# The order of the last sigmoids and of one block's final sums in a fused attention and gated feed-forward kernel

## The chip, the cores and the metric

The kernel runs on one core of one Trainium2 chip. The metric is the device time of one execution in microseconds (us); a lower figure is better. The core's engines work side by side: TensorE (PE) multiplies matrices, with its weight loads shown apart as PEld; VectorE (DVE), ScalarE (ACT) and GpSimd (POOL) do elementwise work; SyncE (SP) issues transfers, as the queues of ACT and POOL can too. Each engine takes its instructions in the order of the program and waits for the others through semaphores.

## The reference

The inputs q, k and v have the shape (8, 8, 576, 64): batch, head, token, head dimension. There are four weight matrices and one vector of gains.

```python
kv  = einsum('bhsd,bhse->bhde', k, v)          # per batch and head, 64 x 64
o   = einsum('bhsd,bhde->bhse', q, kv)
t   = o / sqrt(mean(o * o, -1) + 1e-6)         # per token and head
x   = (t * g_norm), heads side by side         # 4608 tokens x 512
g   = x @ w_gate                               # 512 x 1536
ffn = (gelu(g) * (x @ w_val)) @ w_out          # 1536 x 512
out = x + sigmoid(x @ w_res) * ffn             # float32
```

The result has 4608 rows of 512 numbers. For every one of them the sigmoid's gate multiplies the feed-forward output, and x is added.

## The kernel before, in words

**Blocks.** The tokens are worked on in nine blocks of 512: blocks 0 to 7 hold the first 512 tokens of each of the eight batches, and the last block, number 8, holds the remaining 64 tokens of each batch. A block has four groups of rows j = 0 to 3, each of 128 tokens (one a partition) by 512 columns. For each block there is a stage for gate and value (the hidden rows `hid`, in float16), a stage for the residual gate (`x @ w_res`, kept as a tanh in `th_all`), and the output stage. The attention of later batches is woven in between.

**Fewer products.** From block 1 on, the output stage forms the product with `w_out` in a scheme of seven products instead of eight: rows and columns are halved into quarters, and sums of hidden rows (`hid_s`) and of weights (`wo_ts`) are multiplied. Gate and value (function `gv_group`, from block 2 on in groups of four slices of 128 hidden columns) and, in the last blocks, the residual gate (`res_halves`) are formed in the same way. A product of this kind is written with `prod` or `product`, each into a PSUM bank; intermediate results (called A, D, E, F, c, d) are added by DVE and copied by ACT.

**The final sums.** `out_by_products` makes the output stage of blocks 1 to 7. `pf` (L636) multiplies the gate with the product into `res_all`; the profile calls this tile `osb`. `fin` (L640) adds x, which is in `t_t`, on POOL; `store` (L645) issues the transfer to the output on SP. A pair (jj, ch) names a quarter: jj = 0 is the rows j = 0 and 1, jj = 1 the rows j = 2 and 3; ch is the half of the columns. For block 1 alone (`later`) the sums aren't made at the end of the stage but are put into block 2's first group of gate and value products. They need x there, which at that moment is `t` without the gains: `a_x` (L355) multiplies one group of rows with the gains `g16` on DVE.

**How the work is placed.** The order is written out by hand: `gv_group` runs through a list of words, and `at_word(block, group, word, ...)` hangs further steps behind a word. For a group that is not the block's last one, the list is

```python
False: "1g 1v Eg 5g Ev 5v dg 6g dv 6v Fg 2g Fv 2v 7g g11 7v cg 3g cv 3v h11 g12 4g g21 h12 4v g22 h21 h22",
```

A word with a digit is a product (1 to 7, for gate or value); E and d are copies on ACT (L872, L876), F and c are sums on DVE (L883), g with two digits is a gelu on ACT (L893), h the hidden quarter on DVE, or on POOL for 22 (L899). The two sums `cg` and `cv` read the banks A of gate and value, which the products 4g and 4v write next. Each step is issued at its place to its own engine's queue, so an operation stands behind all that was issued to that engine before.

**The last block.** `out_last` makes the residual gate and the output of block 8. `res_halves` runs through the words `1 sE 5 sd 6 +F 2 tE 7 +c 3 tF 4 tc tA`: digits are products on PE, `sE` and `sd` copies on ACT, `+F` and `+c` sums on DVE, and `tE`, `tF`, `tc`, `tA` tanhs on ACT (L561). `tA` reads the last product in the bank that `wf` takes over. A sigmoid is half a tanh plus one half: `m_sigmoid(j)` (L429) makes it in place for one group of rows of all 512 columns. `half_d(0)` and `half_d(1)` are the two halves of product D; ACT copies D to `d` (L739). Then PE forms the products of A, E, F and A twice more; DVE adds `d` into `wf` (L463), and multiplies each product with its sigmoid (`gated`, L700); `plus` (L704) adds x, on POOL or DVE; `store` (L709) halves each transfer between the SP and the ACT queue. For the lower right quarter, rows j = 2 and 3 of the second half of the columns, POOL forms `u` = sigmoid * d + x ahead (L463, two instructions), and DVE adds it to the gated product (L463).

Of the kernel before, what the change touches and what calls it, by code (L numbers as in the profile page):

```python
# [8 lines left out]
FP32 = mybir.dt.float32  # L9
FP16 = mybir.dt.float16  # L10
I32 = mybir.dt.int32
AF = mybir.ActivationFunctionType
# [6 lines left out]
def kernel(  # L19
# [407 lines left out]
    def m_sigmoid(j):  # L427
        th = th_all[:, j, :]
        nc.scalar.activation(out=th, in_=th, func=AF.Copy, scale=0.5, bias=0.5)  # L429
# [154 lines left out]
    def out_by_products(blk, later, banks, amid):  # L584
        w = {}
        s_ = hid_sums

        def aside(ahead_of):
            for f in amid.get(ahead_of, ()):
                f()  # L590

        def res(jj):
            for j in (2 * jj, 2 * jj + 1):
                m_res(blk, j, banks[j])

        def tiles_of_w():
            for n in ("D", "E", "F", "A"):
                w[n] = pmoe.tile([P, 2, CH], FP32, name="w" + n, bank=banks[n])
            w["d"] = attnp.tile([P, 2, CH], FP32, tag="sq", bufs=3, name="wd")

        def half(n, e, a, b):
            prod(w[n][:, e : e + 1], a, b, e == 0, (e,))

        def half_d(e):
            half("D", e, s_[0], wo_t[:, 0])

        def with_res():
            res_halves(blk, dict(zip("AFE", (banks[j] for j in range(3)))), {
                "sd": [tiles_of_w, lambda: half("A", 0, a_of(blk, 1, 1), b_of(1, 1)), lambda: s_sum(blk, 0)],
                "+F": [lambda: half("A", 1, a_of(blk, 1, 1), b_of(1, 1)), lambda: s_sum(blk, 1),  # L610
                       lambda: nc.scalar.copy(out=w["E"], in_=w["A"])],
                "+c": [lambda: s_sum(blk, 2), lambda: s_sum(blk, 3)],
                "tF": [lambda: half_d(0)],
            })
            half_d(1)
            nc.scalar.copy(out=w["d"], in_=w["D"])
            for j in range(NJ):
                m_sigmoid(j)

        def first_two():  # L620
            tiles_of_w()
            s_last(blk)
            prod(w["A"], a_of(blk, 1, 1), b_of(1, 1), True)
            nc.scalar.copy(out=w["E"], in_=w["A"])
            aside("D")
            prod(w["D"], s_[0], wo_t[:, 0], True)
            nc.scalar.copy(out=w["d"], in_=w["D"])
            aside("gates")
            for j in range(NJ):
                m_sigmoid(j)  # L630

        def part(jj):
            return slice(None), slice(2 * jj[0], 2 * jj[0] + 2), slice(jj[1] * CH, (jj[1] + 1) * CH)

        def pf(jj, src, eng=nc.vector):
            eng.tensor_tensor(out=res_all[part(jj)], in0=th_all[part(jj)], in1=src, op=ALU.mult)  # L636

        def fin(jj):
            of = part(jj)
            nc.gpsimd.tensor_tensor(out=res_all[of], in0=res_all[of], in1=t_t[blk][of], op=ALU.add)  # L640

        def store(jj):
            dst = out[blk * S : blk * S + M0, :].rearrange("(p j) c -> p j c", j=NJ)
            js = slice(2 * jj, 2 * jj + 2)
            nc.sync.dma_start(out=dst[:, js, :], in_=res_all[:, js, :])  # L645

        def others():


            prod(w["A"], s_[1], wo_t[:, 1], False)  # L650
            aside("F")
            sub(nc.vector, w["F"], w["A"], w["d"], ALU.add)
            aside("00")
            prod(w["E"], a_of(blk, 1, 2), b_of(2, 1), False)
            pf((0, 0), w["E"])
            aside("22")
            prod(w["A"], s_[2], wo_t[:, 2], False)
            c22 = res_all[part((1, 1))]
            sub(nc.vector, c22, w["A"], w["d"], ALU.add)
            aside("01")  # L660
            prod(w["F"], s_[3], b_of(2, 2), False)
            pf((0, 1), w["F"])
            aside("11")
            prod(w["A"], a_of(blk, 2, 2), wo_t[:, 3], False)
            if whole(blk + 1):
                pf((1, 1), c22, nc.gpsimd)
                pf((1, 0), w["A"])
            else:
                pf((1, 1), c22)
                pf((1, 0), w["A"])  # L670
            if later:
                return
            for i in (1, 0):
                fin((i, i))
                fin((i, 1 - i))
                store(i)

        if later:
            x = [lambda j=j: a_x(blk, j) for j in range(NJ)]
            at_word(blk + 1, 0, "1v", *x[0:2])  # L680
            at_word(blk + 1, 0, "Fv", x[2])
            at_word(blk + 1, 0, "cv", x[3], lambda: fin((0, 0)), lambda: fin((0, 1)), lambda: store(0))
            at_word(blk + 1, 0, "h22", lambda: fin((1, 0)), lambda: fin((1, 1)), lambda: store(1))
        if res_in_halves(blk):
            return [with_res, lambda: None, lambda: None, others]
        return [lambda: res(0), lambda: res(1), first_two, others]

    def out_last(blk, banks):
# [3 lines left out]
        def bank(n, i):  # L692
            return pmoe.tile([P, n, CH], FP32, name="w", bank=i)

        def part(j, n, ch):
            return slice(None), slice(j, j + n), slice(ch * CH, (ch + 1) * CH)
# [9 lines left out]
        def store(j, n, c0, c1):  # L706
            for e, queue in enumerate((nc.sync, nc.scalar)):
                dst = out.rearrange("(j e s) c -> e s j c", e=2, s=S)[e, M0:S, j : j + n, c0:c1]
                queue.dma_start(out=dst, in_=res_all[e * R : (e + 1) * R, j : j + n, c0:c1])  # L709

        def run():
            wa, w = [], []
            one = (slice(0, 1), slice(1, 2))

            def ahead(e):
                if e == 0:
                    wa.extend(bank(1, banks["A"][e]) for e in range(2))
                    w.extend(bank(2, banks[n]) for n in "DE")
                prod(wa[e], a_of(blk, 1, 1), b_of(1, 1), True, (e,))

            def seed():
                for e in range(2):
                    nc.scalar.copy(out=w[1][:, one[e], :], in_=wa[e])

            def half_d(e):
                prod(w[0][:, one[e], :], s_[0], wo_t[:, 0], e == 0, (e,))

            res_halves(blk, dict(zip("AFE", (banks[j] for j in range(3)))), {
                "sd": [lambda: ahead(0), lambda: s_sum(blk, 0)],
                "+F": [lambda: ahead(1), lambda: s_sum(blk, 1), seed],  # L730
                "+c": [lambda: s_sum(blk, 2), lambda: s_sum(blk, 3)],
                "tF": [lambda: half_d(0)],
            })
            wd, we = w
            wf = bank(2, banks["F"])
            d = attnp.tile([P, 2, CH], FP32, tag="sq", bufs=3, name="wd")
            u = attnp.tile([P, 2, CH], FP32, tag="sq", bufs=3, name="u")
            half_d(1)
            nc.scalar.copy(out=d, in_=wd)  # L739
            for j in (2, 3, 0, 1):  # L740
                m_sigmoid(j)
            for e in range(2):
                prod(wa[e], s_[1], wo_t[:, 1], False, (e,))
                sub(nc.vector, wf[:, one[e], :], wa[e], d[:, one[e], :], ALU.add)
            sub(nc.gpsimd, u, th_all[part(2, 2, 1)], d, ALU.mult)
            sub(nc.gpsimd, u, u, t_t[blk][part(2, 2, 1)], ALU.add)
            prod(we, a_of(blk, 1, 2), b_of(2, 1), False)
            gated(0, 2, 0, we)
            plus(0, 2, 0, nc.gpsimd)
            store(0, 2, 0, CH)  # L750
            prod(wf, s_[3], b_of(2, 2), False)
            gated(0, 2, 1, wf)
            plus(0, 2, 1, nc.gpsimd)
            store(0, 2, CH, C)
            for e in range(2):
                prod(wa[e], s_[2], wo_t[:, 2], False, (e,))
                gated(2 + e, 1, 1, wa[e])
            of = part(2, 2, 1)
            sub(nc.vector, res_all[of], res_all[of], u, ALU.add)
            store(2, 2, CH, C)  # L760
            for e in range(2):
                prod(wa[e], a_of(blk, 2, 2), wo_t[:, 3], False, (e,))
                gated(2 + e, 1, 0, wa[e])
                plus(2 + e, 1, 0, nc.vector)
            store(2, 2, 0, CH)
# [531 lines left out]
    def at_word(blk, i, word, *fs):  # L1297
        amid_gv.setdefault((blk, i), {}).setdefault(word, []).extend(fs)
# [252 lines left out]
```

## Time and profile before

| what | value |
|---|---|
| median of 9 runs | 323.91 us (323.62 to 324.31) |
| the profiled execution's own time | 323.91 us |
| its span, first to last instruction | 322.1 us |
| mean granted clock of TensorE | 0.997 |
| instructions | 7558 |
| last product of PE ends | 315.9 us |
| last DVE operation ends | 318.0 us |

Times of single instructions count from the start of the span. The page of a profile gives the busy time of each engine, a chain of waits followed back from the last instruction, and groups of instructions by line, operation and tile. A group's entry shows the number of instructions, the mean length of one and what ended the idle time before it; the timeline shows them one after the other. An operation's tiles are named by the program: `osb<-osb,t` writes `osb` and reads `osb` and `t`. Some operations go through a helper and bear its line: sums through `sub` are on L463.

### The profile page before, as it was taken

What the parts mean: (1) busy time and instruction counts of PE and PEld (TensorE: products, weight loads), DVE (VectorE), ACT (ScalarE), POOL (GpSimd) and SP (SyncE); (2) the same over time, 40 slices, a digit from 0 to 9 for tenths busy, and PEclk for the clock granted to TensorE, in tenths of its full rate; (3) what the DMA queues carried; (4) which work ended last, traced back from release to release, by engine and by line L of the source; (5) the groups of instructions that cost most, each with busy time, mean ns of one, the idle gap of its engine ahead of it and who ended that gap; (6) DMA issues with size and microseconds to landing.
All of it is one profiled execution on the core that took longest, in us unless ns stands there. A gap on an engine that the chain in (4) does not pass through costs nothing.

```text
span 322.1 us, 7558 instructions
## 1 busy us (share of the span) xinstructions
PE 313.5 (97%) x2972; PEld 240.2 (75%) x2972; DVE 271.5 (84%) x492; ACT 203.7 (63%) x373; POOL 144.9 (45%) x212
## 2 busy tenths in 40 slices
PE   8999999999999999999999999999999999999992
PEld 3545755444857878887888688868888888888881
DVE  5788879799799888998899889999998777877774
ACT  3773685365727784878487848684767467737760
POOL 2792341573712779337843784117511332051232
PEclk9999999999999999999999999999999999999998
DMA  7999999798995599399938893810321030012004
GB/s 254 326 204 204 194 205 182 167 189 124 158 136 102 177 134 96 133 164 120 111 132 160 109 127 131 137 32 2 130 47 36 2 130 4 2 52 80 0 2 130
DMA packets 76693, 38.89 MB, mean 121 GB/s; under 512 B 42098, under 2 KB 74354, under 8 KB 76658
## 3 DMA queue, kind: packets, MB, share of 16 engines
q0 software_dynamic: 38752, 17.17, 42.6%
q1 hardware_dynamic: 37328, 20.71, 24.7%
q8 instruction: 23, 0.38, 0.5%
q10 hardware_dynamic: 578, 0.52, 0.5%
q14 instruction: 12, 0.10, 0.1%
HBM read 38.80 MB, written 9.44 MB: 150 GB/s over the span
## 4 chain that ended last, share of the span: by engine, by line
PE 95%; DVE 3%; issue 0%; ACT 0%; DVEq 0%; ACTq 0%
PE Ag L862 11%; PE Av L862 11%; PE wA L500 11%; PE rps L415 7%; PE gps L395 6%; PE vps L395 6%; PE Fv L862 6%; PE Fg L862 6%; PE fps L432 3%; PE Eg L862 3%; PE wF L500 3%; PE Ev L862 3%; PE wE L500 3%; PE wD L500 3%; PE w L500 2%; PE idle L1027 2%
## 5 line engine op out<-in xcount | busy, mean ns | idle before, releaser
L899 POOL TENSOR_TENSOR hid<-ge,c 128x512 f16<-128x512 f16 x21 | 24.5, 1165 | 68.7 <-ACT ge L893 48.7
L640 POOL TENSOR_TENSOR osb<-osb,t 128x512 f32<-128x512 f32 x28 | 31.5, 1157 | 35.2 <-DVE osb L636 24.3
L500 PEld LDWEIGHTS <-hid_s 128*128 128x128 f16 x384 | 37.6, 98 | 4.3
L862 PEld LDWEIGHTS <-wsv 128*128 128x128 f16 x336 | 32.8, 98 | 4.0
L862 PEld LDWEIGHTS <-wsg 128*128 128x128 f16 x336 | 32.8, 98 | 3.8
L500 PEld LDWEIGHTS <-hid 128*128 128x128 f16 x288 | 28.2, 98 | 4.3
L872 ACT COPY Eg<-Ag 128x512 f32<-128x512 f32 x21 | 12.2, 582 | 25.9 <-PE Ag L862 25.9
L383 ACT ACTIVATE ge<-gps 128x512 f16<-128x512 f32 x24 | 14.1, 597 | 21.3 <-PE gps L395 21.2
L862 PEld LDWEIGHTS <-wg 128*128 128x128 f16 x252 | 24.4, 98 | 3.7 <-issue 0.4
L862 PEld LDWEIGHTS <-wv 128*128 128x128 f16 x252 | 24.6, 98 | 3.3 <-issue 0.2
L883 DVE TENSOR_TENSOR Fg<-Ag,d 128x512 f32<-128x512 f32 x21 | 14.6, 697 | 13.3 <-ACT d L876 7.8
L862 PE MATMUL Ag<-ts,wsg 128*128 128x256 f16 x168 | 25.2, 273 | 0.0
L862 PE MATMUL Av<-ts,wsv 128*128 128x256 f16 x168 | 25.2, 272 | 0.0
L254 DVE TENSOR_REDUCE ss<-sq 128x8 f32<-128x512 f32 x32 | 20.1, 678 | 5.4 <-ACT sq L249 5.4
L395 PE MATMUL gps<-xT,wg 128*128 128x512 f16 x88 | 22.6, 379 | 0.0
L415 PE MATMUL rps<-wr,xT 128*128 128x512 f16 x96 | 22.6, 380 | 0.0
L395 PE MATMUL vps<-xT,wv 128*128 128x512 f16 x88 | 22.6, 379 | 0.0
L500 PE MATMUL wA<-wo_ts,hid_s 128*128 128x256 f16 x168 | 20.6, 273 | 0.0
L384 DVE TENSOR_TENSOR hid<-ge,vps 128x512 f16<-128x512 f16 x24 | 16.2, 683 | 4.8 <-PE vps L395 4.0
L429 ACT ACTIVATE th<-th 128x512 f32<-128x512 f32 x36 | 20.0, 641 | 0.0
L355 DVE TENSOR_TENSOR t<-t,g 128x512 f16<-128x512 f16 x36 | 19.7, 575 | 0.0
L893 ACT ACTIVATE ge<-Eg 128x512 f16<-128x512 f32 x21 | 12.5, 597 | 10.5 <-PE Eg L862 10.5
(209 smaller groups left out, 797.1 us busy)
## 6 DMA issues: line engine op xcount, KB each, us to landing
out_dram<-osb SPq DMA_DIRECT2D x14, 512.0 KB, 2.6
qraw<-in_q_dram POOLq DMA_DIRECT2D x7, 512.0 KB, 7.1
k<-in_k_dram POOLq DMA_DIRECT2D x7, 512.0 KB, 8.6
v<-in_v_dram POOLq DMA_DIRECT2D x7, 512.0 KB, 10.9
wg<-in_moe_w_gate_dram POOLq DMA_DIRECT2D x2, 512.0 KB, 8.2
wv<-in_moe_w_val_dram POOLq DMA_DIRECT2D x2, 512.0 KB, 8.7
wo<-in_moe_w_out_dram POOLq DMA_DIRECT2D x2, 512.0 KB, 13.7
out_dram<-osb SPq DMA_DIRECT2D x4, 256.0 KB, 4.5
```

Source lines behind the costliest of these rows:

```text
L254: nc.vector.tensor_reduce(out=out_, in_=sqs.pop((b, i)), op=ALU.add, axis=mybir.AxisListType.X)
L355: eng.tensor_tensor(out=t_t[blk][:, jj, :], in0=t_t[blk][:, jj, :], in1=g16, op=ALU.mult)
L383: nc.scalar.activation(out=ge, in_=gps, func=AF.Gelu)
L384: nc.vector.tensor_tensor(out=hids[blk][:, f, :], in0=ge, in1=vps, op=ALU.mult)
L395: nc.tensor.matmul(ps[:, j0 * P : j1 * P], lhsT=w[:, cc, :], rhs=xT_t[blk][:, j0:j1, cc, :], start=(cc == 0 and j0 == 0), stop=(cc == NP - ...
L415: nc.tensor.matmul(rps, lhsT=xT_t[blk][:, j, cc, :], rhs=wr16[:, cc, :], start=(cc == 0), stop=(cc == NP - 1),)
L429: nc.scalar.activation(out=th, in_=th, func=AF.Copy, scale=0.5, bias=0.5)
L500: nc.tensor.matmul(ps[:, e - es[0], :], lhsT=a[:, f, e * P : (e + 1) * P], rhs=b[:, f, :], start=(start and e == es[0] and f == 0), stop=( ...
L640: nc.gpsimd.tensor_tensor(out=res_all[of], in0=res_all[of], in1=t_t[blk][of], op=ALU.add)
L862: nc.tensor.matmul(out_[:, r, :], lhsT=lhsT, rhs=rhs, start=(first and r == 0 and c == 0), stop=(c == 1), skip_group_check=True,)
L883: nc.vector.tensor_tensor(out=dst, in0=ps["A", u], in1=sb["d", u], op=ALU.add)
L899: eng.tensor_tensor(out=dst, in0=ge[q], in1=source(q, "v"), op=ALU.mult)
```

## The change

There are two parts.

In the first, the sums of block 1 that stand in block 2's first group are exchanged. Behind the word `cv`, after the fourth multiplication with the gains, there are now the two sums and the store of the rows jj = 1; behind `h22` those of the rows jj = 0.

In the second, the last block's sigmoids are made by quarter (two groups of rows, half of the columns) instead of by group of rows, and in another order. The lower right quarter comes directly behind its tanh `tc`, then the second half of product D and the copy of it to `d`, and only then the tanh `tA`; the other three quarters follow. PE's products keep their order.

```diff
-            at_word(blk + 1, 0, "cv", x[3], lambda: fin((0, 0)), lambda: fin((0, 1)), lambda: store(0))
-            at_word(blk + 1, 0, "h22", lambda: fin((1, 0)), lambda: fin((1, 1)), lambda: store(1))
+            at_word(blk + 1, 0, "cv", x[3], lambda: fin((1, 0)), lambda: fin((1, 1)), lambda: store(1))
+            at_word(blk + 1, 0, "h22", lambda: fin((0, 0)), lambda: fin((0, 1)), lambda: store(0))
...
+            kept = []
+
+            def keep_d():
+                kept.append(attnp.tile([P, 2, CH], FP32, tag="sq", bufs=3, name="wd"))
+                nc.scalar.copy(out=kept[0], in_=w[0])
+
+            def sigmoid(j, ch):
+                th = th_all[part(j, 2, ch)]
+                nc.scalar.activation(out=th, in_=th, func=AF.Copy, scale=0.5, bias=0.5)
+
...
                 "tF": [lambda: half_d(0)],
+                "tc": [lambda: sigmoid(2, 1), lambda: half_d(1), keep_d],
             })
             wd, we = w
+            (d,) = kept
             wf = bank(2, banks["F"])
-            d = attnp.tile([P, 2, CH], FP32, tag="sq", bufs=3, name="wd")
             u = attnp.tile([P, 2, CH], FP32, tag="sq", bufs=3, name="u")
-            half_d(1)
-            nc.scalar.copy(out=d, in_=wd)
-            for j in (2, 3, 0, 1):
-                m_sigmoid(j)
+            for j, ch in ((0, 0), (0, 1), (2, 0)):
+                sigmoid(j, ch)
```

## The prediction

> **What bounds the kernel now.** I read the page first: TensorE (PE) works through nearly the whole span, and of the chain that ended last 95% is PE and 3% VectorE (DVE).
>
> ```profile
> PE 313.5 (97%) x2972; PEld 240.2 (75%) x2972; DVE 271.5 (84%) x492; ACT 203.7 (63%) x373; POOL 144.9 (45%) x212
> PE 95%; DVE 3%; issue 0%; ACT 0%; DVEq 0%; ACTq 0%
> ```
>
> So a change gains only where PE stands still, or behind PE's last product. I asked who waited for whom on PE from 97 us to the end. One line came back:
>
> ```profile
> PE Ag L862 <- DVE c L883: 0.2, 1, 0.2
> ```
>
> The timeline of that place, in block 2's first group of gate and value products (columns: start, length, engine, line, operation; an x2 is two instructions merged), explains it:
>
> ```profile
> 100.26 2.27 POOL L640 TENSOR_TENSOR osb<-osb,t 128x512 f32<-128x512 f32 x2 [10.61 <-DVE t L355]
> 101.54 1.27 DVE L355 TENSOR_TENSOR t<-t,g 128x512 f16<-128x512 f16 x1
> 102.74 0.68 DVE L883 TENSOR_TENSOR c<-Ag,d 128x512 f32<-128x512 f32 x1
> 103.34 0.67 DVE L883 TENSOR_TENSOR c<-Av,d 128x512 f32<-128x512 f32 x1
> 102.69 0.60 PE L862 MATMUL Fv<-xT,wsv 128*128 128x256 f16 x4
> 103.47 0.60 PE L862 MATMUL Ag<-ts,wg 128*128 128x256 f16 x4 [0.18 <-DVE c L883]
> 104.06 0.60 PE L862 MATMUL Av<-ts,wv 128*128 128x256 f16 x4
> 104.50 0.60 PE L862 MATMUL Ag<-xT,wg 128*128 128x256 f16 x4
> ```
>
> PE starts a product of four matmuls every 0.44 us (104.06 to 104.50). From Fv to Ag it takes 0.78, from Ag to Av 0.59: 0.34 + 0.15 = 0.49 us lost. Ag and Av overwrite the banks that the two `c` sums read, and those sums stand behind a multiplication `t<-t,g` that took 1.27 us; the other seven of its kind nearby have a median of 0.416. It ended at 102.81, 0.28 after POOL's pair of adds (100.26 + 2.27 = 102.53).
>
> The second place is the end (timeline again):
>
> ```profile
> 309.41 0.59 ACT L739 COPY wd<-w 128x512 f32<-128x512 f32 x1
> 309.89 2.19 ACT L429 ACTIVATE th<-th 128x512 f32<-128x512 f32 x4
> 311.12 1.28 POOL L463 TENSOR_TENSOR u<-th,wd 128x512 f32<-128x512 f32 x1 [6.91 <-ACT th L429]
> 312.47 1.16 POOL L463 TENSOR_TENSOR u<-u,t 128x512 f32<-128x512 f32 x1
> 313.59 2.27 POOL L704 TENSOR_TENSOR osb<-osb,t 128x512 f32<-128x512 f32 x2
> 313.34 1.08 DVE L700 TENSOR_TENSOR osb<-th,w 128x512 f32<-128x512 f32 x2 [0.54 <-PE w L500]
> 315.17 1.24 DVE L463 TENSOR_TENSOR osb<-osb,u 128x512 f32<-128x512 f32 x1
> 316.33 0.41 DVE L700 TENSOR_TENSOR osb<-th,w 128x256 f32<-128x256 f32 x1
> ```
>
> The chain in order of time leaves PE at 314.62 and then runs on DVE alone to 317.98, before the last stores. Its longest link is the 1.24 us sum at 315.17. An add or multiply of that size with both inputs in SBUF takes 0.68 when POOL is idle:
>
> ```profile
> 90.47 0.68 DVE L636 TENSOR_TENSOR osb<-th,osb 128x512 f32<-128x512 f32 x1
> ```
>
> POOL's last add ran until 313.59 + 2.27 = 315.86; the DVE sum ended 0.55 later, at 316.41.
>
> **What the Trainium skill says.** "SBUF — State Buffer", section "Who interferes with whom": a DVE instruction with two SBUF inputs contends with a POOL instruction that reads SBUF, and the one that comes second blocks fully; with at most one SBUF input outside the two-port modes it does not. The trace agrees with both halves: both long DVE operations have two SBUF inputs and end a fraction after POOL's add, while Fg<-Ag,d (one input in PSUM) took 0.70 during POOL's adds at 100.34, as the sum rF<-rA,rd did at 305.77 with POOL idle. No other page carries a number that I need.
>
> **Part 1, the sums of block 1 in block 2.** Nothing is added or removed: still four POOL adds of 1.16 us and two stores, in the other order. The first pair, rows 1, now also needs the multiplications x[2] and x[3], so it leaves the place where it blocked x[2].
> - x[2] at 101.54 takes about 0.41 instead of 1.27, ending at 101.96. c<-Ag,d waits for its own product: A's four matmuls start at 101.38 and end at 101.98, so it runs from about 102.03 to 102.71; c<-Av,d ends at about 103.3. Ag's natural start is 102.69 + 0.44 = 103.13 and Av's 103.57: both banks are free. All 0.49 us come back. DVE itself regains up to 0.86 us, of which PE needs only this.
> - x[3] ends at about 103.65 (103.94 + 0.41 = 104.35 before). POOL's first pair then runs from 103.7 to 106.0. Queued behind it on POOL are quarter 22 of this group's hidden (before at 105.29; now 106.0 to 107.1), the second pair (107.1 to 109.4) and the next group's quarter 22, whose gelu shifts with PE (110.06 less 0.49 = 109.57). So POOL is back in step by then, with some 0.2 us to spare. The first quarter 22 is 0.65 us later; its reader, the first sum of hidden rows, starts on DVE at 111.11, or 110.6 after the gain: 3.5 us of cover.
> - Between 103.7 and 109.4 DVE has only sums and products with an input in PSUM, so the moved adds block nothing there.
> - SP's queue: the first store stood behind two transposes and went at 105.80; now rows 1 go at about 106.0 and rows 0 at about 109.4 (second store before: 108.7). Landing takes 2.9 to 3.2 us, so by 112.6; these rows are next written at 121.45. Behind them SP has nothing until 128.1. POOL's next loads (112.66) stay behind the second quarter 22.
>
> Part 1: -0.49 us. PE has no further wait named in the trace, so the gain should travel to the end. Bounds: 0 (something later takes it up) to -0.53 (the weight loads' own idle, 0.35 + 0.18).
>
> **Part 2, the last block.** Still four sigmoids of 512 columns, one copy and the same tanhs. ACT's order was tanh rF, rc, rA, copy, four sigmoids; now it is rF, rc, the lower right sigmoid, copy, rA, three sigmoids. PE's order is unchanged.
> - Copy: PE's second half of D starts at 308.55; six matmuls 0.109 apart (18 take 2.13), each 0.27 long, end at 309.37. The copy started at 309.41, so it cannot start earlier. The sigmoid takes the old place of tanh rA: after rc (308.78), about 308.8 to 309.43. The copy ends at about 310.0.
> - POOL's u: from 311.12 to about 310.07, so 1.05 us earlier; u and its second step end at 312.6 instead of 313.63. The two big adds no longer queue behind them: the first waits for DVE's product after PE's w (about 312.06 to 312.75) and runs 312.8 to 313.96; the second waits for the product that ends at 314.02 and runs 314.08 to 315.24, instead of ending at 315.86.
> - DVE's sum still starts at 315.17, since the product before it follows PE. It is then blocked for 0.07 us at most and ends at about 315.86 instead of 316.41: -0.55. Behind it come four DVE instructions, with PE's last halves done at 315.28 and 315.94, before the second product needs its half at about 316.56: the chain moves as a whole. The last stores, issued at 318.01, go at 317.46; SP and ACT are free of the third store by then (it is issued at about 315.95 and takes 0.6 to 0.8).
> - New wait: tanh rA, now behind the copy, ends at about 310.5 instead of 309.35. DVE's two sums into wF write its bank, so the first moves from 310.13 to about 310.55 and the second ends at about 311.37. PE reads wF from 311.83: 0.46 us of cover. DVE's product with w needs only its sigmoid (about 311.05, not 312.08).
>
> Part 2: -0.55 us; bounds 0 (the stores' landing sets the end) and -0.6.
>
> **Sum.** -0.49 - 0.55 = -1.04 us. The profiled execution took 323.91 us (span 322.1 and 1.8 around it), which is also the median of the nine runs. Predicted: 322.87, say 322.9. About 0.2% (0.65 us) is what a measurement of this kernel can tell from no change.
>
> **The cases.**
> - Both gains arrive: 322.6 to 323.15, likeliest 322.9. For it: both stalls have a visible cause and the cover of each moved step is counted. Chance 0.75.
> - Only one arrives: 323.36 or 323.42. Part 1's 0.49 us could be taken up on the way, for the first time at a transposed tile or a load; against it, qrT was issued at 138.1, took 2.8 to land and was read at 142.7, 1.8 us later, and its issue follows PE's progress. Part 2's could vanish in the landing of the stores; against it, the chain view ends on DVE's operations. Chance 0.14.
> - The change does nothing: the two long operations were slow for another cause than POOL. Then 323.9. Against it: both ended a fraction after POOL, and twins without POOL took a third and a half. Chance 0.04.
> - Slower: POOL's backlog in block 2. The next group's quarter 22 has 0.2 us to spare; late, it blocks DVE's sum of hidden rows (two SBUF inputs) and what is queued behind. The first product that reads such a sum (wD, at 117.16) has some 3.4 us of cover (the sum's end is 112.78 + 0.95 = 113.73). It decides only if POOL falls 3.6 us behind; each further microsecond costs one, and 1.7 us beyond that give 324.6. Nothing in the view makes five adds of 1.16 us that long. With anything unseen of that kind: 0.07.
>
> The range 322.6 to 323.45 holds nearly all of the first two cases. Faster 0.76 (nearly all of the first case and a little of the second), same 0.17, slower 0.07.
>
> **What would show it.** In block 2: `t<-t,g` all near 0.41 us, no wait of PE for `c`, POOL's first pair at about 103.7, the second ending at about 109.4. At the end: u at about 310.1, POOL's last add ending at about 315.2, DVE's sum near 0.69 us, the last store issued 0.55 us earlier relative to PE's last product. The prediction is wrong if PE stands still before the wF product, if the sum stays at 1.2 us, or if a new idle stretch appears on PE between 105 and 305 us.

## The result, and the profile after

The changed kernel takes 322.73 us (median of 10 runs, 322.44 to 323.10); the kernel before, with the runs added beside it, 324.01 us (31 runs). The ratio is 0.9961, 95% interval 0.9953 to 0.9969: 1.26 us faster (1.0 to 1.5). The profiled executions took 323.91 and 322.69 us, their spans 322.12 and 320.91.

The page of the changed kernel, busy time and the chain's shares:

```profile
PE 313.2 (98%) x2972; PEld 240.2 (75%) x2972; DVE 270.0 (84%) x492; ACT 203.7 (63%) x373; POOL 144.7 (45%) x212
PE 95%; DVE 3%; issue 0%; ACT 0%; DVEq 0%; ACTq 0%
```

DVE is busy 1.5 us less with the same 492 instructions. From 97 us on the trace no longer names any wait of PE. The timeline of the changed kernel in block 2 (start, length, engine, line, operation; code behind L727 has moved down by nine lines):

```profile
101.56 0.41 DVE L355 TENSOR_TENSOR t<-t,g 128x512 f16<-128x512 f16 x1
...
102.03 0.69 DVE L892 TENSOR_TENSOR c<-Ag,d 128x512 f32<-128x512 f32 x1
...
102.63 0.68 DVE L892 TENSOR_TENSOR c<-Av,d 128x512 f32<-128x512 f32 x1
102.70 0.60 PE L871 MATMUL Fv<-xT,wsv 128*128 128x256 f16 x4
...
103.14 0.60 PE L871 MATMUL Ag<-ts,wg 128*128 128x256 f16 x4
...
103.57 0.60 PE L871 MATMUL Av<-ts,wv 128*128 128x256 f16 x4
103.72 2.27 POOL L640 TENSOR_TENSOR osb<-osb,t 128x512 f32<-128x512 f32 x2 [14.05 <-DVE t L355]
```

x[2], the third of the four multiplications of block 1 with the gains (`t<-t,g` at 101.56), is at 0.41 us, and PE goes from Fv to Ag to Av in steps of 0.44. From the start of x[2] to the end of PE's last matmul it was 315.94 - 101.54 = 214.40 us; now it is 315.45 - 101.56 = 213.89. That is 0.5 us, and nothing on the way took it up.

The timeline of its end:

```profile
308.32 0.63 ACT L736 ACTIVATE th<-th 128x512 f32<-128x512 f32 x1
308.92 0.59 ACT L732 COPY wd<-w 128x512 f32<-128x512 f32 x1
...
309.58 1.27 POOL L463 TENSOR_TENSOR u<-th,wd 128x512 f32<-128x512 f32 x1 [5.85 <-ACT wd L732]
...
312.37 1.15 POOL L704 TENSOR_TENSOR osb<-osb,t 128x512 f32<-128x512 f32 x1 [0.27 <-DVE osb L700]
...
313.68 1.16 POOL L704 TENSOR_TENSOR osb<-osb,t 128x512 f32<-128x512 f32 x1 [0.16 <-DVE osb L700]
...
314.69 0.69 DVE L463 TENSOR_TENSOR osb<-osb,u 128x512 f32<-128x512 f32 x1
```

POOL's two big adds no longer follow one another without a gap: each now waits for DVE. The last ends at 314.83, and the sum takes 0.69 instead of 1.24 us.

The executions differ by some tenths of a microsecond in their opening: x[2] starts between 101.34 and 102.18 in the profiles of this study, though what runs ahead of it is the same but for the POOL work that three of the experiments add. So the end is compared against PE's own end, here and below (us after the end of PE's last matmul; stores as SP issues them):

| kernel | first store | last store | DVE's end | span's end | from last store to the end |
|---|---|---|---|---|---|
| before | -1.16 | 2.08 | 2.05 | 6.18 | 4.10 |
| changed | -1.91 | 1.53 | 1.51 | 5.46 | 3.92 |

The end came 0.72 us nearer to PE's: 0.54 from DVE's chain, 0.18 from the last stores landing sooner after their issue. (One profile can't tell the second figure closely: two experiments that leave the end stage as it was end 6.10 and 6.14 us after PE, where the kernel before shows 6.18.) With 0.5 from block 2 that is the span's 1.21.

### The profile page after: what moved, and what is told of

Its sections match the earlier page's. It is cut to its first block, busy times and chain, and to the rows that moved or that the text cites. A ratio compares the mean times of both kernels' runs of the same rounds, so it can differ in the third digit from the quotient of the medians.

```text
span 320.9 us, 7559 instructions
## 1 busy us (share of the span) xinstructions
PE 313.2 (98%) x2972; PEld 240.2 (75%) x2972; DVE 270.0 (84%) x492; ACT 203.7 (63%) x373; POOL 144.7 (45%) x212
## 4 chain that ended last, share of the span: by engine, by line
PE 95%; DVE 3%; issue 0%; ACT 0%; DVEq 0%; ACTq 0%
PE Ag L871 11%; PE Av L871 11%; PE wA L500 11%; PE rps L415 7%; PE gps L395 6%; PE vps L395 6%; PE Fv L871 6%; PE Fg L871 6%; PE fps L432 3%; PE wF L500 3%; PE Ev L871 3%; PE wE L500 3%; PE wD L500 3%; PE Eg L871 3%; PE w L500 2%; PE idle L1036 2%
## 5 line engine op out<-in xcount | busy, mean ns | idle before, releaser
L355 DVE TENSOR_TENSOR t<-t,g 128x512 f16<-128x512 f16 x36 | 18.8, 552 | 0.0
L341 DVE TENSOR_TENSOR t<-op,ny 128x512 f16<-128x512 f32 x28 | 18.3, 682 | 0.1
```

The lines of the kernel that those rows point to most:

```text
L341: nc.vector.tensor_tensor(out=t, in0=o, in1=scale, op=ALU.mult)
L355: eng.tensor_tensor(out=t_t[blk][:, jj, :], in0=t_t[blk][:, jj, :], in1=g16, op=ALU.mult)
```

## The experiments

**Each part alone.** The first run makes only the exchange in block 2, the second only the edit of the last block.

```diff
 p1_alone: the kernel before, with
-            at_word(blk + 1, 0, "cv", x[3], lambda: fin((0, 0)), lambda: fin((0, 1)), lambda: store(0))
+            at_word(blk + 1, 0, "cv", x[3], lambda: fin((1, 0)), lambda: fin((1, 1)), lambda: store(1))
 ... (and rows 0 behind "h22")
 p2_alone: the changed kernel, with these two lines as before
```

> The kernel before with part 1 alone (rows 1 first in block 2). Blocking theory: PE's 0.49 us at the two products behind the c sums comes back and travels to the end, x[2] takes 0.41 us, the end stage is as before (the sum osb<-osb,u at 1.24 us): 323.5 us, span shorter by 0.5. Rival, that only the end stage gained and the time saved in block 2 is taken up on the way: same as before, 324.0.

> The kernel before with part 2 alone (the last block's sigmoids and the copy). Blocking theory: the sum osb<-osb,u takes 0.69 us instead of 1.24, PE's wait in block 2 stays; the end moves by 0.55 to 0.7 us: 323.3 to 323.5. Rival, that the landing of the last stores sets the end and hides it: same as before, 324.0. If the two parts alone do not add up to the whole change's 1.2 us, they help one another.

Measured: part 1 alone 323.31 us, ratio 0.9980 (0.9970 to 0.9989), 0.65 us faster (0.4 to 1.0); part 2 alone 323.13 us, ratio 0.9982 (0.9974 to 0.9990), 0.58 us faster (0.3 to 0.8). Together 1.23: within these intervals the parts add up to the whole. The profiles are closer: from x[2] to PE's end part 1 alone takes 213.89 us and part 2 alone 214.39, as the changed kernel and the kernel before do to within 0.01. In the profile of part 1 alone PE has no wait left in block 2 and the sum still takes 1.23 us; with part 2 alone PE waits as before, and the end stands at 5.46 us after PE, as in the changed kernel. The rival of one hidden gain falls for both.

**The wait or the order of the rows.** The kernel before keeps its order (rows 0 first), but POOL waits for x[3]:

```diff
-            at_word(blk + 1, 0, "cv", x[3], lambda: fin((0, 0)), ...
+            at_word(blk + 1, 0, "cv", x[3], lambda: nc.gpsimd.tensor_copy(out=hold, in_=t_t[1][0:1, NJ - 1, 0:1]), lambda: fin((0, 0)), ...
```

> The kernel before with its own order of rows, but with a copy of one element on POOL ahead of the first pair of sums that reads the row group of x[3], so that the pair waits for x[3] as it does after the change; part 2 is not made. If it is the wait that helps and not which rows come first: x[2] takes 0.41 us, no wait of PE for c, span shorter by 0.4 to 0.5 as with part 1 alone (POOL some 0.1 us later for the copy). If the order of the rows or of the two stores matters: the 0.49 us do not come, or come in part.

Measured: 323.33 us, ratio 0.9985 (0.9978 to 0.9992), 0.49 us faster, with 323.31 for part 1 alone beside it. Its timeline on DVE and POOL:

```profile
101.59 0.41 DVE L355 TENSOR_TENSOR t<-t,g 128x512 f16<-128x512 f16 x1
...
103.27 0.41 DVE L355 TENSOR_TENSOR t<-t,g 128x512 f16<-128x512 f16 x1
...
103.74 0.18 POOL L682 COPY hold<-t 1x1 f16<-1x1 f16 x1 [14.05 <-DVE t L355]
103.89 1.15 POOL L640 TENSOR_TENSOR osb<-osb,t 128x512 f32<-128x512 f32 x1
```

Rows 0 still come first, and x[2] is free. What helps is that POOL's adds start behind the multiplications; rows 1 first is only a way to make them wait, which needs no instruction.

**Is it POOL's reading?** Three runs add POOL work, whose result nothing uses, to the changed kernel where the kernel before had its first pair of adds. The order stays changed.

```diff
-            at_word(blk + 1, 0, "1v", *x[0:2])
+            at_word(blk + 1, 0, "1v", *x[0:2], lambda: beside())
 beside(): a copy of one element that waits for x[1], then
   pool_read:       two adds scr <- res_all + t, 128x512 float32
   pool_write:      four memsets of scr, 128x512 float32
   pool_read_long:  one add scr <- res_all + t, 128x1024, float16 out
```

> The changed kernel with work added on POOL, whose result nothing uses: behind x[1] in block 2 a copy of one element that waits for x[1], then two adds of 128x512 float32 with both inputs in SBUF, at the place where the kernel before had its first pair (about 100.3 to 102.7). The order of the sums stays changed. Blocking theory: x[2] is blocked again and takes about 1.2 us, PE waits for c again, and some 0.5 us are lost against the changed kernel: 323.2. If the order of the change helped in another way than by keeping POOL still: x[2] at 0.41 us, 322.7.

> As the kernel with two added adds on POOL, but with four memsets of 128x512 float32 in their place: POOL is busy in the same stretch and writes SBUF, but reads nothing there. What the Trainium skill states (a two-input DVE operation is blocked by a POOL instruction that reads SBUF, not by one that only writes): x[2] stays at 0.41 us and the time at the changed kernel's 322.7. If any busy POOL blocks it: x[2] up to 1.2 us, PE waits for c, up to 323.2. If the memsets are over before x[2] starts the run tells nothing; their length isn't in any trace so far.

The run with two adds, pool_read, missed what it was made for: 322.70 us, ratio 0.9955 (0.9941 to 0.9970), as the changed kernel. The second add waits a moment for the first (both write the same tile); the first ends at 101.34, x[2] starts at 101.35 and comes between them. DVE's timeline of this run, then POOL's:

```profile
101.35 0.41 DVE L355 TENSOR_TENSOR t<-t,g 128x512 f16<-128x512 f16 x1
```

```profile
100.20 2.58 POOL L686 TENSOR_TENSOR scr<-osb,t 128x512 f32<-128x512 f32 x2
```

The pair takes 2.58 us where pairs of such adds take 2.27. Taken apart, the first add took 1.14, the gap was 0.08 and the second took 1.36: issued at 101.42, while x[2] ran to 101.77, it was this time POOL that was held up.

With memsets POOL was busy past the whole of x[2]; DVE's timeline, then POOL's:

```profile
101.68 0.41 DVE L355 TENSOR_TENSOR t<-t,g 128x512 f16<-128x512 f16 x1
```

```profile
100.51 2.26 POOL L689 MEMSET scr<- 128x512 f32 x4
```

322.77 us, ratio 0.9955 (0.9939 to 0.9972): no cost. Here x[2] didn't slip into a pause: taken apart, it starts 0.02 us after the third memset and ends within it (101.68 to 102.10 in 101.67 to 102.19), and that memset took 0.525 us like its neighbours. This agrees with "SBUF — State Buffer" of the Trainium skill, "Who interferes with whom": POOL writing alone doesn't block.

> The run with two added adds on POOL again, mended: there x[2] slipped into the 0.08 us between the two. Now one single add of 128x1024 (two float32 inputs in SBUF, a float16 output that nothing uses) starts behind x[1] and should last from about 100.3 to 102.6, past the start of x[2]. The order of the sums stays changed. Blocking theory: x[2] takes about 1.3 us, PE stands still for about 0.5 us ahead of the products behind the c sums, 323.2. If POOL's reading is not the cause: x[2] 0.41 us, 322.7.

With one long add there is no gap to slip into: 323.11 us, ratio 0.9977 (0.9968 to 0.9986), by the medians 0.4 us over the changed kernel, and in the profile the whole 0.5: from x[2] to PE's end it takes 214.40 us again, against 213.89. The timelines of DVE, POOL and PE:

```profile
101.38 1.26 DVE L355 TENSOR_TENSOR t<-t,g 128x512 f16<-128x512 f16 x1
```

```profile
100.23 2.12 POOL L684 TENSOR_TENSOR scr<-osb,t 128x1024 f16<-128x1024 f32 x1
```

```profile
102.52 0.60 PE L878 MATMUL Fv<-xT,wsv 128*128 128x256 f16 x4
103.29 0.60 PE L878 MATMUL Ag<-ts,wg 128*128 128x256 f16 x4 [0.17 <-DVE c L899]
103.89 0.60 PE L878 MATMUL Av<-ts,wv 128*128 128x256 f16 x4
```

x[2] ends 0.29 after POOL (102.64 against 102.35; it was 0.28 before the change), and PE has its stall again, with the rows in the changed order. That an add on POOL which reads SBUF blocks x[2], and a memset doesn't, is shown by putting each in its way.

**The copy's place in part 2.** The copy to `d` goes behind tanh rA again; the lower right sigmoid stays first.

```diff
-                "tc": [lambda: sigmoid(2, 1), lambda: half_d(1), keep_d],
+                "tc": [lambda: sigmoid(2, 1), lambda: half_d(1)],
+                "tA": [keep_d],
```

> The changed kernel with one step of part 2 undone: the copy to d stands behind the tanh of rA again, while the lower right sigmoid stays first. Blocking theory: the copy and with it u start some 0.57 us later (about 310.15), u's second step ends at about 312.66, POOL's two big adds then run without a gap until about 314.98 instead of 314.83; the sum starts at 314.69 and ends 0.55 after POOL, at 315.53, so it takes 0.84 us and the whole costs 0.15 us over the changed kernel: 322.9. Rival, that the sum is slow for the store that is in flight beside it and not for POOL: 0.69 us as in the changed kernel, no cost.

Measured: 322.62 us, ratio 0.9967 (0.9955 to 0.9980). The sum took 0.70 us, and DVE's end stands at 1.51 us after PE and the span's end at 5.47, both as in the changed kernel. My figure of 0.15 was wrong: u starts 0.40 us later against PE's end, not 0.57, and the 0.27 and 0.16 us that POOL otherwise waits before its two big adds take that up. POOL's last add ends 0.62 us before PE's end in both. The copy's place is worth nothing that can be seen here: the sigmoids by quarter, with the lower right one first, are enough for the gain of part 2.

A rival stands in the expectation: that the sum was slow for the store in flight beside it and not for POOL. The transfers settle it. In the kernel before, the busy share of the DMA engines from 312 us on was (40 slices of 0.28 us):

```profile
DMA  0000000000000007999489999966995000000000
```

The stores' first data move at 316.1 us, when the slow sum had been running since 315.17. In the changed kernel they move from 314.9 us on (its row stands further down), beside a sum of 0.69 us, and in the run chain_late, further down too, the sum takes 0.68 us with the stores flowing. POOL's add wasn't put back beside the sum by itself; that POOL blocked it rests on part 2's runs, on the end of the slow sum 0.55 us after POOL's add in every profile that has it (1.22 to 1.24 us), and on what block 2 showed.

**What sets the end: DVE's chain or the transfers?** Part 2 moved the first store by 0.75 us against PE, DVE's end by 0.54 and the end by 0.72, so the store's start could be the cause as well. Two runs moved one without the other.

```diff
 first_store_joined: the changed kernel, one store for two
-            store(0, 2, 0, CH)
...
-            store(0, 2, CH, C)
+            store(0, 2, 0, C)
 chain_late: the changed kernel, DVE's chain put back
             of = part(2, 2, 1)
+            sub(nc.vector, d[:, :, 0:192], u[:, :, 0:192], u[:, :, 0:192], ALU.add)
             sub(nc.vector, res_all[of], res_all[of], u, ALU.add)
```

> The changed kernel with the first store of the last block's upper rows not issued after POOL's first big add but joined with the second one, as one store of both halves of the columns after the second add, 1.3 us later. DVE's and POOL's work is as in the changed kernel. Theory that DVE's chain sets the end (it ends 1.51 us after PE, the last store goes 0.03 later): no cost, 322.7. Rival, that what set the end was when the first store starts, since part 2 moved it by 0.74 us against PE's end and the end by 0.72, but DVE's end by only 0.54: 0.4 us or more is lost, 323.1 and more.

> The changed kernel with one more DVE operation (an add of 128x384 float32 into d, whose result nothing uses) ahead of the sum osb<-osb,u. It puts DVE's chain, the third and the last store back by about 0.55 us, to where they stood against PE's end before the change, while the first two stores stay early. If DVE's chain sets the end: the end moves back by 0.5 to 0.55 us against PE's end, 323.2. If the pace of the transfers from the first store on sets it: 0.2 us or less, 322.7 to 322.9.

| kernel | first store | last store | DVE's end | span's end | from last store to the end | median, ratio (95% interval) |
|---|---|---|---|---|---|---|
| changed | -1.91 | 1.53 | 1.51 | 5.46 | 3.92 | 322.73, 0.9961 (0.9953 to 0.9969) |
| first_store_joined | -0.59 | 1.54 | 1.51 | 6.60 | 5.05 | 324.03, 0.9996 (0.9987 to 1.0006) |
| chain_late | -1.91 | 2.00 | 1.97 | 5.96 | 3.96 | 323.12, 0.9973 (0.9965 to 0.9981) |

Both matter. With DVE's chain and the two stores behind it 0.46 us later and the first stores where they were, the end is 0.50 later: a delay of the chain comes out at the end. With the chain untouched and the first store 1.3 us later, the end is 1.14 later: all that the change had brought is gone. The transfers from 312 us on (busy share of the DMA engines and GB/s, in 40 slices of 0.28 us), first of the changed kernel, then of the joined store:

```profile
DMA  0000000000298975999999388960000000000000
GB/s 0 0 0 0 0 0 0 0 0 0 63 209 149 291 242 164 190 242 309 335 238 372 93 212 186 279 238 0 0 0 0 0 0 0 0 0 0 0 0 0
```

```profile
DMA  0000000000000003989989999999982000000000
GB/s 0 0 0 0 0 0 0 0 0 0 0 0 0 0 0 89 231 171 209 164 209 283 294 272 268 298 339 309 305 283 89 0 0 0 0 0 0 0 0 0
```

The same 1.05 MB go out. In the changed kernel the DMA engines run nearly dry for a moment (the 3 in the row, 93 GB/s) just before the last store's data come. Behind the joined store they are full to the end, and on ACT's queue the third and the last store take 1.15 and 1.50 us to issue instead of 0.81 and 0.63: the last store queues. The joined store also has a form of its own (256 KB in rows twice as long), so its 1.14 us aren't the price of the delay alone; how much the delay alone costs isn't shown.

**Three attempts to end sooner.** Knowing this, I tried to take more from the end. One run put the sum on POOL and merged DVE's adds, one only merged the adds, and one merged the adds and moved the first big add to DVE.

```diff
 sum_on_pool:
-            sub(nc.vector, res_all[of], res_all[of], u, ALU.add)
+            sub(nc.gpsimd, res_all[of], res_all[of], u, ALU.add)
 sum_on_pool, merge_plus and first_store_early:
                 gated(2 + e, 1, 0, wa[e])
-                plus(2 + e, 1, 0, nc.vector)
+            plus(2, 2, 0, nc.vector)
 first_store_early:
-            plus(0, 2, 0, nc.gpsimd)
+            plus(0, 2, 0, nc.vector)
```

> The changed kernel with the end drawn up for the same rule: the sum osb<-osb,u goes to POOL behind its last add (about 314.83 to 316.0), and DVE makes its two products first and then one add of 128x512 for both, instead of product, add, product, add. Blocking theory: DVE's products have an input in PSUM and pass (about 314.86 to 315.27 and 315.51 to 315.92); the add with two SBUF inputs is blocked until POOL ends at 316.0 and ends 0.55 later, at 316.55 instead of 316.96: 0.4 us faster, 322.3. Rival: POOL's sum starts late or runs long, or the store of that quarter, now 0.6 us later, lands last: no gain or a loss, 322.7 or more.

> The changed kernel with DVE's last four operations (product, add, product, add, of 256 columns each) as three: two products, then one add of 128x512. The sum and all stores but the last keep their times. If DVE's chain sets the end: 0.81 + 0.69 us instead of 1.58 with its waits, the last store is issued about 0.19 us earlier and the end with it, 322.55. If the transfers' own pace sets it: the last store goes earlier but lands no earlier, 322.7.

> The changed kernel with the merged last add of the earlier run, and with the first big add of the upper rows on DVE instead of POOL: 0.69 instead of 1.16 us and no hand-over, in a stretch where DVE is idle for 0.62 us. The first store goes about 0.5 us earlier; the product behind the add, POOL's other add and the second store go about 0.08 later, DVE's chain ends about 0.1 earlier than in the changed kernel. If the transfers set the end: 0.3 to 0.5 us earlier than the changed kernel, 322.3. If DVE's chain does: 0.1, 322.6.

| kernel | first store | third store | last store | DVE's end | span's end | median, ratio (95% interval) |
|---|---|---|---|---|---|---|
| changed | -1.91 | 0.12 | 1.53 | 1.51 | 5.46 | 322.73, 0.9961 (0.9953 to 0.9969) |
| sum_on_pool | -1.90 | 0.64 | 1.32 | 1.18 | 5.55 | 322.67, 0.9954 (0.9935 to 0.9972) |
| merge_plus | -1.91 | 0.12 | 1.34 | 1.32 | 5.40 | 322.81, 0.9960 (0.9948 to 0.9972) |
| first_store_early | -2.42 | 0.13 | 1.35 | 1.32 | 5.34 | 322.42, 0.9961 (0.9949 to 0.9972) |

With the sum on POOL, DVE ends 0.33 us earlier, yet the span's end is 0.09 later. The third store is issued 0.52 later, the last one waits 0.14 for SP's queue behind it and then takes 4.2 us to the end of the span instead of 3.92. Merging brings 0.19 us on DVE and 0.06 at the end, so a shorter chain doesn't bring at the end what a longer one cost there. A first store 0.51 us earlier brings another 0.06: from here on an earlier start is worth little; why isn't shown. So sum_on_pool and merge_plus didn't gain the 0.4 and 0.19 us expected if the chain alone set the end, nor first_store_early the 0.3 to 0.5 expected if the transfers did; its 0.12 in all is near the 0.1 expected for the chain, but merge_plus, with the same end of DVE, has only half of that. None of the three can be told from the changed kernel by its ratio; the last has the lowest median, and the nearest end in the profile.

## Why the prediction was right

Forecast was 322.9 us in a range of 322.6 to 323.45, measured is 322.73; of a gain, 1.04 us were forecast, and the profiles show 1.21. By its steps:

- **Part 1, -0.49.** Measured 0.5, from x[2] to PE's end. Each time came as worked out: x[2] ending at 101.97 (101.96 forecast), the first c sum from 102.03, POOL's pair from 103.72 (103.7), its last add of block 1 ending at 109.35 (109.4), the next quarter 22 at 109.57 (109.57). The backlog on POOL, the rival that ends slower, never reached anyone.
- **Part 2, -0.55, bounds 0 and -0.6.** Measured 0.72: the mechanism was right, the size was not, and it lay outside the bounds. DVE's part came as forecast, 0.54. Right were (moved by PE's 0.48 us) the copy at 309.41, u at 310.07, the sum starting at 315.17 and no longer blocked, and the sum into wF from 310.52 (310.55). The mis-sized term is the landing of the last store, which I carried over unchanged behind its issue: 4.10 us from the issue to the end before, 3.92 after. The profiles with part 2's early stores and nothing else moved at the end have 3.91 to 3.93, those without it 4.03 to 4.10. It is bound up with the other transfers, as the joined store shows with 5.05. With DVE's chain late but the first stores early it is 3.96, so most of the sooner landing goes with the early stores rather than with the shorter chain; why it is just 0.18 isn't taken apart by these runs.
- **Only one gain arrives, or none.** Each part alone gave its own time, so both fall. "The chain view ends on DVE's operations" was a weak reason against the transfers: the gain did arrive, but the joined store lost everything with an unchanged chain on DVE.
- **The place of the copy** stood in my working as a part of the 1.05 us by which u comes earlier. It did move u, by 0.40 us, but POOL had that to spare.

## What to carry to other kernels

Where a DVE operation with two inputs in SBUF is far longer than its twins and ends a fraction after a POOL operation that reads SBUF, move one of the two out of the other's way; what the move is worth is read where PE or the last store waits for that DVE operation. A change of order that makes POOL wait for the right thing can be enough, without a further instruction; the wait itself, made with one small copy, did the same here. At a kernel's end, look at two things: when the last store is issued, and what the stores before it still have on the DMA engines by then.

## What the runs showed of the hardware that I had not expected

- The blocked operation doesn't start from nothing when POOL ends: the float16 multiplication of 0.41 us ended 0.28 to 0.29 after POOL's add, the float32 sum of 0.68 ended 0.55 after. Both figures are 0.13 us short of the operation's own length, so an overlap of about 0.13 us is free. With 0.14 to 0.15 of overlap, in the changed kernel and with the late copy, the sum took 0.69 to 0.70, with 0.16, in first_store_early, 0.71.
- Who comes second is held up, on either engine: in pool_read, POOL's add took 1.36 instead of 1.14 us when issued 0.07 us behind a DVE operation of 0.41 us. That is one case.
- A pause of 0.08 us between two POOL adds is enough for the DVE operation to go between them. In the kernel before there was no such pause: the second add was issued 0.04 us before the first had ended, x[2] came 0.13 us after the first's end, and it was the second add that it waited for. The same goes for the sum at the end.
